# Lightning attention and a GELU MLP on one core: the first four MLP blocks by single chunks, VectorE rounding the first weights, chunk 2 transposed behind them

## The chip, the cores and the metric

The kernel runs on one NeuronCore of one Trainium2 chip. The metric is the time on the device in microseconds (us). TensorE (PE) multiplies matrices, VectorE (DVE) and ScalarE (ACT) work element by element and empty the accumulators (PSUM), GpSimd (POOL) issues the loads that change the type from f32 to bf16 and does a few products, SyncE (SP) issues the other transfers.

## The reference

Linear attention with a decay per head, in blocks of 64 rows, and then an MLP with an exact GELU over all heads of a token:

```python
    for b in range(nb):
        intra = np.einsum('bhic,bhjc->bhij', qb, kb) * Dmask[None]
        intra = np.einsum('bhij,bhjd->bhid', intra, vb)
        inter = np.einsum('bhid,bhde->bhie', qb * lam_pow[None], kv_state)
        out[:, :, sl] = intra + inter
        kv_state = lam_block[None, :, None, None] * kv_state + np.einsum('bhsd,bhse->bhde', kb_dec, vb)
    ...
    h = x @ w_in
    g = 0.5 * h * (1.0 + erf(h * inv_sqrt2))
    return (g @ w_out).astype(np.float32)
```

q, k and v are 4 x 8 x 768 x 64 (batch, heads, rows, width); x is 3072 x 512, w_in 512 x 2048, w_out 2048 x 512, all f32.

## The kernel before

The rows are cut into chunks of 128 rows of one batch with all heads: 24 chunks, numbered so that chunks 0 to 3 are the first rows of the four batches. Four chunks make a group; there are six groups. For each chunk k and q are transposed on PE (`transposed`, L165), their product gives the scores (`scores`, L191), DVE multiplies these by a mask that holds the decay (`masked`, L202), and the product with v gives the attention's output (`outputs`, L222), which ACT or DVE copies as bf16 into the chunk's 128 columns of the group's `x_t` (`empty_outputs`, L237). `next_state` (L206) multiplies k by the decayed v (`decay_v`, L160, on POOL) and DVE makes the state for the next chunk of that batch from it; its accumulator has the tag "t", of which there is one bank.

The MLP of a group (`mlp_blocks`, L398) is a list of blocks. A first-layer block `mm1(kf, ks, cols)` makes, for `ks` slices of 128 of the 2048 hidden columns, the product of w_in with the columns `cols` of `x_t`, four matmuls of that width for each slice, into a bank with the tag "mh" (two of them, shared with the transposes of k), and ACT applies GELU from there. In group 0 the plan (L437 to L440) goes by what of x exists: blocks of two chunks first, then the third alone, then three chunks, the fourth alone, and four. `group0` (L546) says before which block a step of attention stands; PE executes all in the order in which it is written. The head (L481 to L516) does chunks 0 and 1 and chunk 2's transposes; between the steps it has products of zeros (`keep_warm`, L465) that nobody reads, in a bank with the tag "mo" (two, shared with the transposes of q).

The order on the queues matters too. POOL issues the loads in the order of L94 (`k0 q0 v0 k1 q1 v1 w1 k2 ...`, where w1 to w7 are pairs of slices of w_in), then the decayed v of chunks 0 to 2, w_out and the further loads. The first two slices of w_in come another way: SP loads them as f32 into `wide_w` (L75), and ACT rounds them into `w_in_t` (L500). On DVE, the decay table (L125), its mask (L479, `causal`), the copies of transposes out of PSUM and the masked scores follow each other in the order of the text.

Behind group 0's first layer stand its second layer (L421), between whose parts the attention of chunks 4 to 7 lies (`e + 8` to `e + 15`), and DVE's sums of w_out (`w_out_sums`, L263), which the later groups use.

Of the kernel before, what the change touches and what calls it, by code (L numbers as in the profile page):

```python
# [15 lines left out]
def kernel(  # L16
# [10 lines left out]
    nc = tc.nc  # L27
# [3 lines left out]
    C = 128  # L31
# [8 lines left out]
    M = 4  # L40
# [33 lines left out]
    wide_w = sum_pool.tile([128, NK1, 256], F32, tag="g1", name="wide_w")  # L74
# [7 lines left out]
    w_in_t = w_pool.tile([128, NK1, d_ff], BF16)  # L82
# [65 lines left out]
    xT = {}  # L148
    states = {}

    def bank(shape, dtype, tag, name):
        return ps.tile(shape, dtype, tag=tag, name=name, bufs=2 if tag in ("sc", "mh", "mo") else 1)
# [12 lines left out]
    def transposed(c, name, tag, empty):  # L165

        src, t_ps = getattr(c, name), bank([128, HP, C], BF16, tag, "t_ps")
        for hp in range(HP):
            nc.tensor.transpose(t_ps[:, hp, :], src[:, 2 * hp:2 * hp + 2, :], ident)  # L169
        dst = work_pool.tile([128, HP, C], BF16, tag=name + "T", name=name + "T")  # L170
        setattr(c, name + "T", dst)
        empty(dst, t_ps)  # L172
# [18 lines left out]
    def scores(c):  # L191
        sc_ps = [bank([128, HP, C], F32, "sc", f"sc_ps{hi}") for hi in range(2)]
        for hp in range(HP):
            for hi in range(2):
                p = slice(hi * D, (hi + 1) * D)
                nc.tensor.matmul(sc_ps[hi][:, hp, :], c.kT[p, hp, :], c.qT[p, hp, :], start=True, stop=True)  # L196
        c.sc_m = work_pool.tile([128, HP, 2, C], BF16, tag="sc_m", name="sc_m")
        c.sc_ps = sc_ps
        for hi in range(0 if c.n == 0 else 2):
            masked(c, hi)  # L200

    def masked(c, hi):  # L202
        mask = decay[:, hi] if c.early else cmask[:, None, :].to_broadcast((128, HP, C))
        nc.vector.tensor_mul(c.sc_m[:, :, hi, :], c.sc_ps[hi], mask)  # L204

    def next_state(c):  # L206
        if c.sb == NB - 1:
            return
        kv_ps = bank([128, HP, 128], F32, "t", "kv_ps")
        for hp in range(HP):  # L210
            nc.tensor.matmul(kv_ps[:, hp, :], c.k[:, 2 * hp:2 * hp + 2, :], c.v_dec[:, 2 * hp:2 * hp + 2, :],  # L211
                             start=True, stop=True)
        new = work_pool.tile([128, HP, 128], BF16, tag="state_f", name="state", bufs=8)
        if c.sb == 0:
            nc.vector.tensor_mul(new, kv_ps, lam_blk)
        else:
            tmp = work_pool.tile([128, HP, 128], F32, tag="tmp", name="tmp")
            nc.vector.tensor_add(tmp, kv_ps, states[c.n])  # L218
            nc.vector.tensor_mul(new, tmp, lam_blk)  # L219
        states[c.n + M] = new  # L220

    def outputs(c, x_t, off, evacuate=True):  # L222
        o_ps = bank([128, HP, C], F32, "o", "o_ps")
        if c.sb > 0:
            for hp in range(HP):
                nc.tensor.matmul(o_ps[:, hp, :], states[c.n][:, hp, :], c.qT[:, hp, :],  # L226
                                 start=(hp == 0), stop=False, skip_group_check=True)
        v = c.v if c.early else c.v_dec
        for hi in range(2):
            for hp in range(HP):  # L230
                nc.tensor.matmul(o_ps[hi * D:(hi + 1) * D, hp, :], v[:, 2 * hp + hi, :], c.sc_m[:, hp, hi, :],  # L231
                                 start=(c.sb == 0 and hp == 0), stop=True, skip_group_check=True)
        c.x_o, c.o_ps = x_t[:, :, off * C:(off + 1) * C], o_ps
        if evacuate:
            empty_outputs(c)

    def empty_outputs(c):  # L237
        if c.n < 2 * M:
            nc.scalar.copy(c.x_o, c.o_ps)
        else:  # L240
            nc.vector.tensor_mul(c.x_o, c.o_ps, lam_q)  # L241
# [151 lines left out]
        blocks += [((lambda f=f, u=u: f(u)), KH * DH) for f in (m3, m4, m5, m2, m1, m6, m7) for u in range(2)]  # L393
        return blocks

    N1 = 21

    def mlp_blocks(g):  # L398
        T = M * C
        x_t = xT[g]  # L400
        g_t = g_pool.tile([128, NK2, T], BF16, tag="g", name="g_t")

        def mm1(kf, ks=1, cols=slice(0, T)):
            n = cols.stop - cols.start

            def run():
                h_ps = bank([128, ks, n], F32, "mh", "h_ps")
                parts = [(0, T - C), (T - C, T)] if g == 1 and kf == 0 else [(0, n)]
                for k in range(ks):
                    for lo, hi in parts:  # L410
                        for ki in range(NK1):
                            nc.tensor.matmul(h_ps[:, k, lo:hi], w_in_t[:, ki, (kf + k) * 128:(kf + k + 1) * 128],  # L412
                                             x_t[:, ki, cols.start + lo:cols.start + hi],
                                             start=(k == 0 and lo == 0 and ki == 0), stop=(ki == NK1 - 1),
                                             skip_group_check=True)
                nc.scalar.activation(g_t[:, kf:kf + ks, cols], h_ps, ACT.Gelu)  # L416
            return run

        om = {}

        def mm2(io, part):  # L421
            def run():
                if part == 0:
                    om[io] = bank([128, d_model], F32, "mo", "o2_ps")
                for kf in range(part * 4, part * 4 + 4):
                    nc.tensor.matmul(om[io], g_t[:, kf, io * C:(io + 1) * C], w_out_t[:, kf, :],  # L426
                                     start=(kf == 0), stop=(kf == NK2 - 1))
                if part == NK2 // 4 - 1:
                    o_sb = out_pool.tile([128, d_model], F32, tag="o_s", name="o_sb")
                    nc.scalar.copy(o_sb, om[io])  # L430
                    nc.sync.dma_start(out_r[g, :, io, :], o_sb)
            return run

        parts = NK2 // 4
        if g > 0:
            return blocks_by_seven(g, g_t, [(mm1(kf), 4 * T) for kf in range(NK2)])
        two, three, third, fourth = slice(0, 2 * C), slice(0, 3 * C), slice(2 * C, 3 * C), slice(3 * C, T)  # L437
        plan = [(kf, 1, two) for kf in range(6)] + [(0, 4, third), (4, 2, third)]
        plan += [(kf, 1, three) for kf in range(6, 12)] + [(kf, 4, fourth) for kf in range(0, 12, 4)]
        plan += [(kf, 1, slice(0, T)) for kf in range(12, NK2)]  # L440
        assert len(plan) == N1
        blocks = [(mm1(kf, n, cols), 4 * n * (cols.stop - cols.start)) for kf, n, cols in plan]
        blocks += [(mm2(io, part), 4 * 512) for pair in range(0, M, 2) for part in range(parts)
                   for io in (pair, pair + 1)]
        return blocks
# [15 lines left out]
    live = {}  # L461
# [3 lines left out]
    def keep_warm(n, new=True, cols=256):  # L465

        if new:
            idle_ps[0] = bank([128, 512], F32, "mo", "idle_ps")
        for _ in range(n):
            nc.tensor.matmul(idle_ps[0][:, :cols], idle[:, :128], idle[:, :cols], start=True, stop=True)  # L470

    def early(n):
        live[n] = begin(n, early=True)
        return live[n]

    copy = nc.vector.tensor_copy
# [4 lines left out]
    make_powers()  # L481
    nc.scalar.activation(warm, pos, ACT.Gelu)
    keep_warm(11, cols=512)
    c = early(0)
    causal(0)
    transposed(c, "k", "mh", copy)
# [7 lines left out]
    c = early(1)  # L494
# [2 lines left out]
    keep_warm(3, new=False)  # L497
    transposed(c, "q", "mo", copy)
    outputs(live[0], xT[0], 0)
    nc.scalar.copy(w_in_t[:, :, :256], wide_w)  # L500
    keep_warm(2)
    scores(c)
    keep_warm(9, new=False)
    make_lam_blk()
    outputs(live[1], xT[0], 1)
    c = early(2)
    transposed(c, "k", "mh", copy)
    transposed(c, "q", "mo", copy)
    keep_warm(1)
    for n in range(3):  # L510
        decay_v(live[n], nc.gpsimd)
    for s in range(2):
# [28 lines left out]
    def both_transposed(c):  # L541
        transposed(c, "k", "mh", nc.vector.tensor_copy)
        transposed(c, "q", "mo", nc.vector.tensor_copy)

    e = N1
    group0 = {  # L546
        1: [lambda: scores(live[2])],
        5: [lambda: outputs(live[2], xT[0], 2)],
        6: [lambda: next_state(live[0])],
        7: [lambda: next_state(live[1])],  # L550
        8: [lambda: both_transposed(live[3])],
        9: [lambda: next_state(live[2])],
        10: [lambda: scores(live[3])],
        12: [lambda: outputs(live[3], xT[0], 3)],
        17: [lambda: next_state(live[3])],
        e: [w_out_sums, lambda: decay_v(live[4], nc.vector)],
        e + 8: [lambda: transposes(live[4])],
        e + 9: [lambda: scores(live[4])],
# [10 lines left out]
    for n in range(2 * M, NCH):  # L569
        g, i = n // M - 1, n % M  # L570
        first, apart = (0.21, 0.2) if g == 1 else (0.06, 0.245)
# [65 lines left out]
```

## Time and profile before

| what | value |
|---|---|
| time, median of 3 runs | 209.86 us (209.69 to 210.2) |
| profiled execution, its own time | 209.99 us |
| its span in the profile | 208.2 us |
| PE busy | 200.3 us, 96% of the span |
| granted PE clock | 0.998 |
| POOL's issue of a load of k, q or v | about 0.9 us, 128 KB each |

A line of the timeline gives the start, the length, the engine, the line of the kernel, the operation with what it writes and reads, the count, and in brackets how long the engine had been idle and what ended that. Matmuls overlap, so the time from one start to the next is what one costs, and not its length. In the chain of waits each step is followed back to what released it.

### The profile page before, as it was taken

What the parts mean: (1) busy time and instruction counts of PE and PEld (TensorE: products, weight loads), DVE (VectorE), ACT (ScalarE), POOL (GpSimd) and SP (SyncE); (2) the same over time, 40 slices, a digit from 0 to 9 for tenths busy, and PEclk for the clock granted to TensorE, in tenths of its full rate; (3) what the DMA queues carried; (4) which work ended last, traced back from release to release, by engine and by line L of the source; (5) the groups of instructions that cost most, each with busy time, mean ns of one, the idle gap of its engine ahead of it and who ended that gap; (6) DMA issues with size and microseconds to landing.
All of it is one profiled execution on the core that took longest, in us unless ns stands there. A gap on an engine that the chain in (4) does not pass through costs nothing.

```text
span 208.2 us, 4142 instructions
## 1 busy us (share of the span) xinstructions
PE 200.3 (96%) x1708; PEld 130.5 (63%) x1725; DVE 139.0 (67%) x220; ACT 81.7 (39%) x145; POOL 97.1 (47%) x112
## 2 busy tenths in 40 slices
PE   7889999999999999999999999999999999999992
PEld 2457574465555788654688554688555688544881
DVE  4744525855476789889779689579678579123482
ACT  4966563324555410265420265410365410466200
POOL 8999953799998995499300493000200000000000
PEclk9999999999999999999999999999999999999999
DMA  5999999999999999999930699100651000500014
GB/s 116 155 174 177 200 207 188 154 215 148 151 177 154 153 150 154 233 141 175 155 25 3 219 134 175 29 0 3 227 103 29 0 0 3 201 0 0 3 50 151
DMA packets 102370, 24.65 MB, mean 118 GB/s; under 512 B 92880, under 2 KB 99536, under 8 KB 102352
## 3 DMA queue, kind: packets, MB, share of 16 engines
q0 software_dynamic: 80688, 13.37, 90.2%
q1 hardware_dynamic: 21664, 11.02, 23.5%
q8 instruction: 13, 0.21, 0.4%
q14 instruction: 5, 0.04, 0.1%
HBM read 27.27 MB, written 6.29 MB: 161 GB/s over the span
## 4 chain that ended last, share of the span: by engine, by line
PE 86%; POOL 8%; DVE 3%; issue 1%; POOLq 0%; DVEq 0%
PE h_ps L412 39%; PE p_ps L306 9%; PE r_ps L306 8%; PE q_ps L306 8%; PE o_ps L426 7%; PE o_ps L231 4%; PE s_ps L306 3%; PE sc_ps L196 3%; PE kv_ps L211 3%; POOL w_in_t L88 3%; PE o_ps L226 2%; POOL k_t L67 2%; POOL q_t L67 2%; POOL v_t L67 2%; PE t_ps L169 1%
## 5 line engine op out<-in xcount | busy, mean ns | idle before, releaser
L416 ACT ACTIVATE g_t<-h_ps 128x512 bf16<-128x512 f32 (+2 forms) x101 | 58.2, 576 | 81.2 <-PE h_ps L412 81.0
L412 PE MATMUL h_ps<-x_t,w_in_t 128*128 128x512 bf16 (+3 forms) x446 | 88.7, 343 | 0.6
L412 PEld LDWEIGHTS <-w_in_t 128*128 128x128 bf16 x460 | 40.2, 98 | 36.0 <-issue 0.6
L163 POOL TENSOR_TENSOR v_dec<-v_t,lam_m 128x512 bf16<-128x512 bf16 x23 | 25.2, 1101 | 44.5 <-PE kv_ps L211 42.9
L306 PEld LDWEIGHTS <-g_sum 128*128 128x128 bf16 x400 | 38.6, 98 | 5.2
L281 DVE TENSOR_TENSOR g_sum<-g_t 128x1024 bf16<-128x1024 bf16 x50 | 33.6, 716 | 11.3 <-ACT g_t L416 11.3
L204 DVE TENSOR_TENSOR sc_m<-sc_ps,cmask 128x512 bf16<-128x512 f32 x40 | 25.6, 680 | 2.0 <-PE sc_ps L196 2.0
L67 POOL DMA_DIRECT2D v_t<-in_v_dram x24 | 21.4, 893 | 3.3 <-DMA w_out_t<-in_moe_w_out_dram 2.9
L67 POOL DMA_DIRECT2D k_t<-in_k_dram x24 | 22.2, 924 | 1.7 <-DMA w_out_t<-in_moe_w_out_dram 1.4
L67 POOL DMA_DIRECT2D q_t<-in_q_dram x24 | 21.6, 898 | 2.1 <-DMA w_out_t<-in_moe_w_out_dram 2.1
L306 PE MATMUL r_ps<-w_sum,g_sum 128*128 128x256 bf16 x160 | 19.3, 273 | 0.1
L241 DVE TENSOR_TENSOR x_t<-o_ps,lam_q 128x512 bf16<-128x512 f32 x16 | 11.0, 687 | 10.2 <-PE o_ps L231 10.2
L306 PEld LDWEIGHTS <-g_t 128*128 128x128 bf16 x160 | 15.3, 98 | 3.2
L218 DVE TENSOR_TENSOR tmp<-kv_ps,state 128x512 f32<-128x512 f32 x16 | 11.0, 689 | 7.8 <-PE kv_ps L211 7.8
L426 PE MATMUL o_ps<-w_out_t,g_t 128*128 128x512 bf16 x61 | 14.8, 380 | 0.1
L219 DVE TENSOR_TENSOR state<-tmp,lam_blk 128x512 bf16<-128x512 f32 x16 | 14.4, 901 | 0.5
L306 PE MATMUL p_ps<-w_sum,g_t 128*128 128x256 bf16 x80 | 10.1, 273 | 0.0
L196 PE MATMUL sc_ps<-qT,kT 64*128 64x128 bf16 x192 | 9.5, 218 | 0.3 <-DVE qT L172 0.3
L306 PE MATMUL q_ps<-w_sum,g_t 128*128 128x256 bf16 x80 | 9.7, 273 | 0.0
L470 PE MATMUL idle_ps<-idle 128*128 128x256 bf16 (+1 forms) x33 | 8.4, 393 | 1.2 <-DVE idle L101 1.2
L426 PEld LDWEIGHTS <-g_t 128*128 128x128 bf16 x64 | 5.8, 98 | 6.1
L306 PE MATMUL p_ps<-w_out_t,g_sum 128*128 128x256 bf16 x80 | 9.6, 273 | 0.0
(65 smaller groups left out, 168.0 us busy)
## 6 DMA issues: line engine op xcount, KB each, us to landing
out_dram<-o_sb SPq DMA_DIRECT2D x9, 512.0 KB, 2.8
k_t<-in_k_dram POOLq DMA_DIRECT2D x24, 128.0 KB, 5.9
q_t<-in_q_dram POOLq DMA_DIRECT2D x24, 128.0 KB, 6.1
v_t<-in_v_dram POOLq DMA_DIRECT2D x24, 128.0 KB, 6.2
w_out_t<-in_moe_w_out_dram POOLq DMA_DIRECT2D x4, 512.0 KB, 11.1
w_in_t<-in_moe_w_in_dram POOLq DMA_DIRECT2D x7, 256.0 KB, 7.5
out_dram<-o_sb SPq DMA_DIRECT2D x5, 256.0 KB, 5.7
wide_w<-in_moe_w_in_dram SPq DMA_DIRECT2D x1, 512.0 KB, 4.2
```

Of the source, the lines that this page charges most:

```text
L67: nc.gpsimd.dma_start(raw[n, name], chunk_of(name, n))
L163: eng.tensor_mul(c.v_dec, c.v, lam_m[:, :, None].to_broadcast((128, H, D)))
L196: nc.tensor.matmul(sc_ps[hi][:, hp, :], c.kT[p, hp, :], c.qT[p, hp, :], start=True, stop=True)
L204: nc.vector.tensor_mul(c.sc_m[:, :, hi, :], c.sc_ps[hi], mask)
L218: nc.vector.tensor_add(tmp, kv_ps, states[c.n])
L219: nc.vector.tensor_mul(new, tmp, lam_blk)
L241: nc.vector.tensor_mul(c.x_o, c.o_ps, lam_q)
L281: nc.vector.tensor_tensor(gsum[i][:, ks, :], g_t[:, ka + k:ka + k + n4, ta], g_t[:, kb + k:kb + k + n4, tb], op=op)
L306: nc.tensor.matmul(o, left[i](k, slice(u * C, (u + 1) * C)), right[i](k), start=(begin and k == 0), stop=(k == KH - 1), skip_group_check=True)
L412: nc.tensor.matmul(h_ps[:, k, lo:hi], w_in_t[:, ki, (kf + k) * 128:(kf + k + 1) * 128], x_t[:, ki, cols.start + lo:cols.start + hi], start ...
L416: nc.scalar.activation(g_t[:, kf:kf + ks, cols], h_ps, ACT.Gelu)
L426: nc.tensor.matmul(om[io], g_t[:, kf, io * C:(io + 1) * C], w_out_t[:, kf, :], start=(kf == 0), stop=(kf == NK2 - 1))
```

## The change

The plan of group 0 begins with blocks of one chunk: two of two slices for the first chunk, one of four slices for the second; the blocks of two chunks are left for slices 4 and 5. The plan has 20 blocks in place of 21. Block 0 now stands before chunk 1's outputs, and block 1 behind them. Chunk 2 is transposed behind block 2, and its scores stand before block 3. The idle matmuls are 15 in these places, where there were 10. The rounding of `wide_w` is a DVE copy ahead of chunk 0's transposes, and no longer an ACT copy behind chunk 0's outputs. Of the steps further on, the first state now stands behind the third chunk's block of four slices (it stood ahead of it) and the second behind the third chunk's block of two slices, right ahead of chunk 3's transposes; the others keep their place in the work, by the new numbers of blocks.

```diff
-    N1 = 21
+    N1 = 20
...
-        two, three, third, fourth = slice(0, 2 * C), slice(0, 3 * C), slice(2 * C, 3 * C), slice(3 * C, T)
-        plan = [(kf, 1, two) for kf in range(6)] + [(0, 4, third), (4, 2, third)]
+        two, three = slice(0, 2 * C), slice(0, 3 * C)
+        first, second, third, fourth = (slice(i * C, (i + 1) * C) for i in range(M))
+        plan = [(0, 2, first), (2, 2, first), (0, 4, second)] + [(kf, 1, two) for kf in range(4, 6)]
+        plan += [(0, 4, third), (4, 2, third)]
...
     keep_warm(11, cols=512)
+    copy(w_in_t[:, :, :256], wide_w)
     c = early(0)
...
     outputs(live[0], xT[0], 0)
-    nc.scalar.copy(w_in_t[:, :, :256], wide_w)
     keep_warm(2)
     scores(c)
-    keep_warm(9, new=False)
     make_lam_blk()
-    outputs(live[1], xT[0], 1)
-    c = early(2)
-    transposed(c, "k", "mh", copy)
-    transposed(c, "q", "mo", copy)
-    keep_warm(1)
+    early(2)
...
-        1: [lambda: scores(live[2])],
-        5: [lambda: outputs(live[2], xT[0], 2)],
+        0: [lambda: keep_warm(2)],
+        1: [lambda: keep_warm(2), lambda: outputs(live[1], xT[0], 1)],
+        3: [lambda: both_transposed(live[2]), lambda: keep_warm(5), lambda: scores(live[2]),
+            lambda: keep_warm(6, new=False)],
+        4: [lambda: outputs(live[2], xT[0], 2)],
         6: [lambda: next_state(live[0])],
-        7: [lambda: next_state(live[1])],
-        8: [lambda: both_transposed(live[3])],
-        9: [lambda: next_state(live[2])],
-        10: [lambda: scores(live[3])],
-        12: [lambda: outputs(live[3], xT[0], 3)],
-        17: [lambda: next_state(live[3])],
+        7: [lambda: next_state(live[1]), lambda: both_transposed(live[3])],
+        8: [lambda: next_state(live[2])],
+        9: [lambda: scores(live[3])],
+        11: [lambda: outputs(live[3], xT[0], 3)],
+        16: [lambda: next_state(live[3])],
```

## The prediction, made before the changed kernel ran

> **What bounds the kernel now.** The page comes first: the engines' shares and the chain that ended last.
>
> ```profile
> PE 200.3 (96%) x1708; PEld 130.5 (63%) x1725; DVE 139.0 (67%) x220; ACT 81.7 (39%) x145; POOL 97.1 (47%) x112
> PE 86%; POOL 8%; DVE 3%; issue 1%; POOLq 0%; DVEq 0%
> ```
>
> TensorE (PE) carries the chain but for 8% of POOL, which is the head: the chain in order of time runs over POOL's load issues from 1.38 us to the end of the first decayed v at 18.53, and on PE from there. So the edits count by what they do to PE's order of work in the head, and a change there is worth what is left of it at the next point that does not move with PE. Next the timeline of PE, from 10.8 to 22 us (start, length, engine, line, what, count, idle before):
>
> ```profile
> 11.04 1.16 PE L470 MATMUL idle_ps<-idle 128*128 128x256 bf16 x9
> 12.12 0.74 PE L231 MATMUL o_ps<-sc_m,v_t 128*64 128x128 bf16 x8
> 13.42 0.40 PE L169 MATMUL t_ps<-ident,k_t 128*128 128x128 bf16 x4 [0.56 <-DMA k_t<-in_k_dram]
> 14.25 0.40 PE L169 MATMUL t_ps<-ident,q_t 128*128 128x128 bf16 x4 [0.44 <-DMA q_t<-in_q_dram]
> ...
> 18.79 1.06 PE L412 MATMUL h_ps<-x_t,w_in_t 128*128 128x128 bf16 x16
> 19.81 0.40 PE L211 MATMUL kv_ps<-v_dec,k_t 128*128 128x128 bf16 x4
> 20.04 0.61 PE L412 MATMUL h_ps<-x_t,w_in_t 128*128 128x128 bf16 x8
> 20.53 0.38 PE L169 MATMUL t_ps<-ident,k_t 128*128 128x128 bf16 x4
> 20.75 0.39 PE L169 MATMUL t_ps<-ident,q_t 128*128 128x128 bf16 x4
> 21.12 0.81 PE L412 MATMUL h_ps<-x_t,w_in_t 128*128 128x384 bf16 x4
> ```
>
> The hole that the change fills is seen here: from 11.04 to 14.60 PE does nine idle matmuls, chunk 1's outputs and chunk 2's transposes, and waits 1.0 us for k and q of chunk 2. The mark to measure against is 21.12, the first block of three chunks: up to there both orders hold the same useful work (blocks 0 to 5 for two chunks, the same six for the third, two states, chunk 3's transposes), and behind it they go on alike.
>
> Then the timelines of DVE and ACT, which set when PE's inputs are there:
>
> ```profile
> 4.16 1.29 DVE L125 TENSOR_TENSOR decay<-dist,ln 128x512 f32<-128x512 f32 x2 [1.69 <-ACT ln L121]
> 6.10 0.69 DVE L479 TENSOR_TENSOR decay<-decay,cmask 128x512 f32<-128x512 f32 x1 [0.65 <-ACT decay L126]
> 6.71 0.42 DVE L172 COPY kT<-t_ps 128x512 bf16<-128x512 bf16 x1
> 7.59 0.42 DVE L172 COPY qT<-t_ps 128x512 bf16<-128x512 bf16 x1 [0.46 <-PE t_ps L169]
> ...
> 11.14 1.29 DVE L204 TENSOR_TENSOR sc_m<-sc_ps,decay 128x512 bf16<-128x512 f32 x2 [0.58 <-PE sc_ps L196]
> ```
>
> ```profile
> 10.99 1.05 ACT L500 CAST w_in_t<-wide_w 128x1024 bf16<-128x1024 f32 x1
> 11.94 0.81 ACT L143 COPY lam_blk<-lam_c 64x256 f32<-64x256 f32 x2
> 12.90 0.59 ACT L239 CAST x_t<-o_ps 128x512 bf16<-128x512 f32 x1
> ```
>
> DVE has 0.65 and 0.46 us of slack early on, and the second part of x is there at 13.49.
>
> Last, what does not move with PE (timeline of all engines around 40 us):
>
> ```profile
> 39.57 0.69 DVE L163 TENSOR_TENSOR v_dec<-v_t,lam_m 128x512 bf16<-128x512 bf16 x1 [0.16 <-DMA v_t<-in_v_dram]
> 40.18 0.68 DVE L175 TENSOR_TENSOR qT<-t_ps,lam_q 128x512 bf16<-128x512 bf16 x1
> 40.91 0.40 PE L196 MATMUL sc_ps<-qT,kT 64*128 64x128 bf16 x8
> ```
>
> Chunk 4's scores start 0.05 after qT is done at 40.86; qT stands behind a decayed v that waited for a load, and DVE's eight sums of w_out before it run without a pause from 34.40, when w_out landed. PE is ready at about 40.9 as well (the matmul before is issued at about 40.59 and takes 0.22 to the next, and a change to this form costs 0.09). So whatever PE gains before that is lost in front of these scores; what it loses is kept.
>
> **The change, part by part.** Start to start on PE, read off the rows: 0.056 us for a matmul of 128 columns, 0.109 for 256, 0.22 for four transposes; 0.33 to 0.35 for eight of scores or outputs with the change of form around them.
>
> *Rounding on DVE.* 128x1024 f32 to bf16. No such copy is in the trace: from below, twice the PSUM copies of 512 (0.42, of which 0.34 to the next) make 0.7 to 0.8, and 0.69 if only the part by element doubles; from above, f32 products run 0.69 and 0.60 more per 512, so 1.29. I take 0.75: one source, as the copy has. It starts at 5.45, when the decay products are done; wide_w is then there (issued 1.20, 4.2 to landing: 5.40). At 0.75 it ends at 6.20 and moves the mask product by 0.1, at 1.29 by 0.6; kT's copy follows, and qT's waits for q until 7.59 anyway, so 0.46 more of slack: nothing, or 0.1 at the upper end. Without that cover it would cost its whole length, as all of DVE up to the mask of chunk 0 stands behind it. On ACT 1.05 us falls away at 10.99; nothing waited for ACT there.
>
> *Blocks 0 to 2.* Chunk 1's scores leave PE at 11.04 as before. Two idle matmuls (0.23), block 0 (8 x 0.056 = 0.45; x's first part is done at 11.10), two idle ones: 11.94. Chunk 1's outputs wait for the second mask at 12.43, as before, and leave PE at 12.80. Block 1 needs w_in's second load (6.77 + 5.8 = 12.57): 13.25. Block 2 needs x's second part, 13.49: it starts at 13.55, waits 0.30, and ends at 14.44 (16 x 0.056).
>
> *Chunk 2.* Transposes 14.47 to 14.92 (k and q are there by 14.21); DVE's two copies end at 15.67. Five idle matmuls end at 15.5, scores start at 15.73 (wait 0.23) against 15.17 before. Six idle matmuls: 16.73. Block 3 (4 x 0.109 = 0.44, its load there at 10.13 + 6.3 = 16.43): 17.16. Outputs wait for the mask (16.15 + 1.29 = 17.44) and leave PE at 17.84. Block 4: 18.28. Block 5 reads x's third part: ACT copies it from 17.94 to 18.53, so 18.59 (wait 0.31) to 19.48.
>
> *States and chunk 3.* First state's matmuls 19.48 to 19.71; its v came at 18.53. Block 6 (0.45): 20.16. The second state needs the one kv bank, which DVE frees 0.69 after 19.98, at 20.67: 20.73 (wait 0.57; before, a block of 16 lay between and the wait was 0.1). With its four and the eight transposes: 21.41, and the first block of three chunks at 21.44.
>
> **The sum:** 21.44 - 21.12 = **+0.3 us**. Of the hole's idle time, five more idle matmuls (15 for 10, 0.55) and four new waits (0.30 + 0.23 + 0.31 + 0.57 = 1.41) take back all that the early blocks win. Behind 21.4 the loads leave room (the w_in load for blocks 8 and 9 is issued at 14.21 and takes 7.5: 21.7, needed at 23.4), and the order is the old one. At 40.9 up to 0.05 of it goes unseen. The profiled execution took 209.99 (span 208.2 and 1.8 around it), 0.13 above the median of the three, 209.86; the span becomes 208.5, and against the median I say **210.15**.
>
> **A rule against it.** The row: DVE and POOL do hold each other up in this trace; a sum of g took 1.40 for its usual 0.68 at 77.48, while POOL multiplied v from 77.26 to 78.32. POOL's issue of k at 1.38 took 1.06 for the later 0.88 to 0.90, beside DVE's constants. The Trainium skill (SBUF — State Buffer, section on SBUF's two separate sides) says that an f32 copy within SBUF on VectorE locks GpSimd out of a shared port, so that a DMA issued by GpSimd cannot write its descriptors. By that rule the time would be that of the first rival below. By another of its pages (VectorE: DVE Perf Modes, the perf-mode tier table) 2048 such elements take 1.23 us, so that some 0.7 is an estimate for 1024; the sum would be the same.
>
> **Rivals.**
> *POOL held by the copy (slower).* The copy runs in the middle of POOL's issue of chunk 1's q and v (5.05 and 5.91, 0.9 each, back to back). q lands at 9.65 (4.6 after its issue) and is transposed at 9.70: no slack; chunk 1's scores and outputs, x's second part and block 2 all hang on it, and later loads queue behind. If POOL stands for the copy's length, all moves by up to 0.75, the loads before 40.9 too: 209.86 + 0.3 + 0.3 to 0.75 = 210.5 to 210.9, say **210.75**. It decides from about 0.35 us of stall. For it: the rows above. Against: issue runs 4.6 us ahead of landing, so the transfers may have enough queued.
> *The copy comes late (slower at the edge).* wide_w is 0.05 ahead of its use; 0.3 later and 1.29 long, the copy ends near 7.0, qT's comes 0.3 later and masks and outputs with it: **210.4**.
> *The waits do not arise (faster).* Were the four waits absent, PE would reach the mark at 20.35, 0.8 early: **209.1**. That needs the loads of w_out and v before 40.9 to come earlier too, or the gain stays in front of chunk 4's scores; the row of 39.57 speaks against it.
>
> **How the numbers follow.** Forecast 0.46, its own range 209.8 to 210.5; POOL held 0.30; copy late 0.10; faster 0.14. A measurement of this kernel can tell about 0.3% (0.63 us) from no change: faster is under 209.23, slower over 210.49. Faster 0.13 (nearly all of its rival), slower 0.34 (most of POOL held, half of copy late, little of the forecast), same 0.53. The range, 209.2 to 210.95, leaves out the far half of each side's rival.
>
> **What would show it.** The first block of three chunks at 21.4; waits of PE ahead of block 2, block 5, chunk 2's scores and the second state near 0.3, 0.3, 0.2 and 0.6; DVE's copy at 5.45 and 0.7 to 0.8 long; POOL's issues at 5.05 and 5.91 still 0.9. Wrong if these issues last over 1.2, if chunk 1's q is transposed after 10.0, or if chunk 4's scores start before 40.8.

## The result, and the profile after

| kernel | median, us | lowest to highest | middle half of the runs |
|---|---|---|---|
| before (22 runs) | 209.89 | 209.66 to 210.54 | 209.75 to 209.97 |
| changed (22 runs) | 210.38 | 209.89 to 211.87 | 210.11 to 210.60 |

The ratio is 1.0025, with an interval of 1.0013 to 1.0037: 0.5 us slower (0.3 to 0.8), which is under the 0.3% that was named as the bound of "same". What the medians do not say is in the last column: in these runs the changed kernel scatters twice as much. The profiled execution of the changed kernel is one of its quickest, 209.99 with a span of 208.2, as before; that of the kernel before lies a little above its median. So the two profiles cannot show the difference of the medians.

PE's timeline after the change, for the stretch that was shown of before:

```profile
10.64 0.40 PE L196 MATMUL sc_ps<-qT,kT 64*128 64x128 bf16 x8
10.97 0.39 PE L472 MATMUL idle_ps<-idle 128*128 128x256 bf16 x2
11.20 0.61 PE L412 MATMUL h_ps<-x_t,w_in_t 128*128 128x128 bf16 x8
11.64 0.38 PE L472 MATMUL idle_ps<-idle 128*128 128x256 bf16 x2
11.96 0.84 PE L231 MATMUL o_ps<-sc_m,v_t 128*64 128x128 bf16 x8
12.87 1.65 PE L412 MATMUL h_ps<-x_t,w_in_t 128*128 128x128 bf16 x24
14.36 0.39 PE L169 MATMUL t_ps<-ident,k_t 128*128 128x128 bf16 x4
14.58 0.39 PE L169 MATMUL t_ps<-ident,q_t 128*128 128x128 bf16 x4
14.81 0.71 PE L472 MATMUL idle_ps<-idle 128*128 128x256 bf16 x5
15.59 0.40 PE L196 MATMUL sc_ps<-qT,kT 64*128 64x128 bf16 x8
15.92 0.83 PE L472 MATMUL idle_ps<-idle 128*128 128x256 bf16 x6
16.77 0.61 PE L412 MATMUL h_ps<-x_t,w_in_t 128*128 128x256 bf16 x4
17.31 0.43 PE L231 MATMUL o_ps<-sc_m,v_t 128*64 128x128 bf16 x8
17.67 1.81 PE L412 MATMUL h_ps<-x_t,w_in_t 128*128 128x256 bf16 x20
19.32 0.39 PE L211 MATMUL kv_ps<-v_dec,k_t 128*128 128x128 bf16 x4
19.54 0.61 PE L412 MATMUL h_ps<-x_t,w_in_t 128*128 128x128 bf16 x8
20.56 0.40 PE L211 MATMUL kv_ps<-v_dec,k_t 128*128 128x128 bf16 x4 [0.41 <-DVE state L215]
...
21.24 0.81 PE L412 MATMUL h_ps<-x_t,w_in_t 128*128 128x384 bf16 x4
```

The hole after 11 us is filled, and another has opened: between chunk 2's transposes and block 3 (14.81 to 16.77) PE does eleven idle matmuls and the scores, where the kernel before did a block, the scores and then four blocks of two chunks, which covered the masks of DVE. The second state waits for the kv bank: eight matmuls from 19.54 need 0.45, the state starts at 20.56. The first block of three chunks, the mark, comes at 21.24 for 21.12; counted from chunk 1's scores it is 10.60 us for 10.41.

DVE's and POOL's timelines around the copy:

```profile
5.33 1.13 DVE L486 CAST w_in_t<-wide_w 128x1024 bf16<-128x1024 f32 x1
6.38 0.67 DVE L481 TENSOR_TENSOR decay<-decay,cmask 128x512 f32<-128x512 f32 x1
6.97 0.41 DVE L172 COPY kT<-t_ps 128x512 bf16<-128x512 bf16 x1
7.47 0.42 DVE L172 COPY qT<-t_ps 128x512 bf16<-128x512 bf16 x1
```

```profile
5.03 0.90 POOL L67 DMA_DIRECT2D q_t<-in_q_dram  x1
5.90 1.04 POOL L67 DMA_DIRECT2D v_t<-in_v_dram  x1
6.92 0.77 POOL L88 DMA_DIRECT2D w_in_t<-in_moe_w_in_dram  x1
```

The copy is long (1.13), the mask product behind it comes at 6.38 for 6.10, and qT's copy finds its slack and is not late. POOL's issue of chunk 1's v takes 1.04 for 0.91.

Why the two profiled executions have the same span although the mark is 0.12 later is seen in DVE's timeline at 77 us, first before, then after:

```profile
77.48 1.40 DVE L281 TENSOR_TENSOR g_sum<-g_t 128x1024 bf16<-128x1024 bf16 x1
...
82.40 0.67 DVE L376 TENSOR_TENSOR f_x<-f_x,r_ps 128x512 f32<-128x512 f32 x1
```

```profile
77.61 0.68 DVE L281 TENSOR_TENSOR g_sum<-g_t 128x1024 bf16<-128x1024 bf16 x1
...
81.81 0.67 DVE L376 TENSOR_TENSOR f_x<-f_x,r_ps 128x512 f32<-128x512 f32 x1
```

The sum of g met POOL's product of v before (1.40) and did not after (0.68). DVE's last step, for which PE waits, ends 0.6 earlier, and PE's next product starts at 83.06 for 83.12: that execution got back 0.18 there. The experiments below bear this out: from chunk 4's scores to that product it takes 42.21 to 42.32 in the five profiles in which this sum met the product of v in full (before, e6, e8, e9, e11), and 42.03 to 42.05 in the eight others, e5 left aside. Four of the five have the order of before, seven of the eight that of the changed kernel; whether the order brings this about was not tried.

### The profile page after: what moved, and what is told of

Its sections match the earlier page's. It is cut to its first block, busy times and chain, and to the rows that moved or that the text cites. A ratio compares the mean times of both kernels' runs of the same rounds, so it can differ in the third digit from the quotient of the medians.

```text
span 208.2 us, 4199 instructions
## 1 busy us (share of the span) xinstructions
PE 200.9 (96%) x1746; PEld 131.0 (63%) x1746; DVE 141.8 (68%) x221; ACT 80.6 (39%) x143; POOL 97.2 (47%) x112
## 3 DMA queue, kind: packets, MB, share of 16 engines
q0 software_dynamic: 80688, 13.37, 92.5%
q1 hardware_dynamic: 21664, 11.02, 23.2%
## 4 chain that ended last, share of the span: by engine, by line
PE 91%; DMA 3%; POOL 3%; DVE 1%; ACT 0%; issue 0%; POOLq 0%; DVEq 0%
PE h_ps L412 40%; PE r_ps L306 9%; PE p_ps L306 9%; PE q_ps L306 8%; PE o_ps L426 7%; PE s_ps L306 4%; PE o_ps L231 4%; PE sc_ps L196 4%; DMA w_in_t<-in_moe_w_in_dram 3%; PE kv_ps L211 2%; PE o_ps L226 2%; PE t_ps L169 1%; POOL k_t L67 1%; POOL v_t L67 1%; POOL q_t L67 1%
## 5 line engine op out<-in xcount | busy, mean ns | idle before, releaser
L412 PE MATMUL h_ps<-x_t,w_in_t 128*128 128x512 bf16 (+3 forms) x476 | 90.2, 338 | 0.2
L281 DVE TENSOR_TENSOR g_sum<-g_t 128x1024 bf16<-128x1024 bf16 x50 | 34.9, 743 | 10.7 <-ACT g_t L416 10.7
L219 DVE TENSOR_TENSOR state<-tmp,lam_blk 128x512 bf16<-128x512 f32 x16 | 15.0, 939 | 0.5
L426 PE MATMUL o_ps<-w_out_t,g_t 128*128 128x512 bf16 x64 | 15.3, 380 | 0.0
```

Of the source, the lines that this page charges most:

```text
L281: nc.vector.tensor_tensor(gsum[i][:, ks, :], g_t[:, ka + k:ka + k + n4, ta], g_t[:, kb + k:kb + k + n4, tb], op=op)
```

## The experiments

Theory 1: the DVE copy holds POOL, and the blocks hang on the loads behind it. Theory 2: PE's new order costs, the copy nothing. Theory 3, formed after the first four kernels: the kernel before hides delays of the head in waits that end when a load or POOL is done; the changed one hands them on. "Mark" is the start of the first block of three chunks. The kernel before has a median of 209.84 to 209.88 in the three sets, beside the same kernels. The ratios and intervals are those on record, to the kernel before; a ratio need not be that of the two medians, as a few runs far out count in it.

**e1: the rounding back on ScalarE.** The changed kernel, with

```diff
     nc.scalar.activation(warm, pos, ACT.Gelu)
+    nc.scalar.copy(w_in_t[:, :, :256], wide_w)
     keep_warm(11, cols=512)
-    copy(w_in_t[:, :, :256], wide_w)
```

> The changed kernel with one part moved: ScalarE rounds wide_w, right behind its warm-up GELU at 9.9 us, and DVE does not. Theory 1 (the DVE copy holds POOL's issue, and blocks 1 and 3 hang on the loads behind it): POOL's issue of chunk 1's v is back at 0.91 us (1.04 in the changed kernel), w_in's second load lands near 12.5 (12.8), the third near 16.4 (16.7), block 3 starts at 16.5 or before; the first block of three chunks at 21.0 (21.24); the time 0.2 to 0.4 us below the changed kernel's 210.4, with less scatter. Theory 2 (only PE's new order costs; the copy is free): the loads land as in the changed kernel, or sooner without PE following; time within 0.1 of 210.4.

Median 210.34, ratio to before 1.0023 (1.0001 to 1.0045), mark at 21.23. POOL's issue is back at 0.91, and the time has not followed. In this execution w_in's second load, on which block 1 hangs, also landed 1.0 us sooner (issued at 6.78 and 5.0 us on its way, for 6.92 and 5.9), and the mark stayed.

**e2: the DVE copy alone, in the kernel before.**

```diff
     keep_warm(11, cols=512)
+    copy(w_in_t[:, :, :256], wide_w)
...
-    nc.scalar.copy(w_in_t[:, :, :256], wide_w)
```

> The kernel before, with one part of the change alone: DVE rounds wide_w ahead of chunk 0's transposes, ScalarE does not. Theory 1: POOL's issue of chunk 1's v takes 1.0 us or more, loads from there on land 0.2 to 0.3 later, chunk 2's transposes (which wait for k and q at 13.4 and 14.25) move by as much, and the first block of three chunks comes at 21.3 to 21.4 for 21.12: time 210.1 to 210.3. Theory 2: nothing moves by more than 0.1; time 209.8 to 210.0.

Median 209.96, ratio 1.0003 (0.9972 to 1.0033), mark at 21.13. The issue is 1.04 long here too. The interval is wide, but e1 and e2 agree: theory 1 falls. PE's timeline of e2 showed something else:

```profile
13.68 0.40 PE L169 MATMUL t_ps<-ident,q_t 128*128 128x128 bf16 x4 [0.39 <-DMA q_t<-in_q_dram]
...
18.57 0.38 PE L211 MATMUL kv_ps<-v_dec,k_t 128*128 128x128 bf16 x4 [0.63 <-POOL v_dec L163]
...
21.13 0.81 PE L412 MATMUL h_ps<-x_t,w_in_t 128*128 128x384 bf16 x4
```

In this execution chunk 2's q came 0.57 earlier than in the profile of before (13.68 for 14.25), and nothing came of it: the first state waited for POOL until 18.57, the same time as before. Hence theory 3.

**e3: without the eleven idle matmuls.** The changed kernel, with

```diff
-        3: [lambda: both_transposed(live[2]), lambda: keep_warm(5), lambda: scores(live[2]),
-            lambda: keep_warm(6, new=False)],
+        3: [lambda: both_transposed(live[2]), lambda: scores(live[2])],
```

> The changed kernel without the five and the six idle matmuls around chunk 2's scores (nothing else). Theory 1: block 3 waits for w_in's third load, which lands at 16.7, so it still starts at 16.75 and the time stays at 210.3 to 210.5. Theory 2 (the idle matmuls stand on the path): block 3 starts at 16.05 and the mark comes 0.3 to 0.6 earlier; time 209.8 to 210.1. If the granted clock falls below 0.99 in the first 20 us, the idle matmuls were needed and neither can be read.

Median 210.10, ratio 1.0011 (0.9987 to 1.0035), granted clock 1.0. In the profiled execution PE waits in place of doing the idle matmuls, 0.62 for DVE's copies ahead of the scores and 0.73 for the load ahead of block 3, and the mark stays (21.25):

```profile
16.76 0.61 PE L412 MATMUL h_ps<-x_t,w_in_t 128*128 128x256 bf16 x4 [0.73 <-DMA w_in_t<-in_moe_w_in_dram]
```

So here the load bounds block 3, as expected by theory 1, but it does not bound the mark. In all seven profiles with this order up to there, e5 left aside (the changed kernel, e1, e3, e4, e7, e10, e11), block 4 starts 2.07 to 2.08 after chunk 2's scores, whether block 3 starts 0.76 (e11) or 1.18 (the changed kernel) after them: chunk 2's outputs behind block 3 wait for DVE's masks. The idle matmuls and the load both fit into that wait. The median lies at the upper edge of what theory 2 expected, and the mark where theory 1 had it; the interval is too wide for the median to decide.

**e4: the states' order.** The changed kernel, with

```diff
-        7: [lambda: next_state(live[1]), lambda: both_transposed(live[3])],
-        8: [lambda: next_state(live[2])],
-        9: [lambda: scores(live[3])],
+        7: [lambda: both_transposed(live[3]), lambda: next_state(live[1])],
+        9: [lambda: next_state(live[2]), lambda: scores(live[3])],
```

> The changed kernel with the order around the states changed: chunk 3's transposes ahead of the second state, the third state one block later, right ahead of chunk 3's scores. Theory 2 (the wait of 0.58 us of the second state for the one kv bank is on the path): the wait falls under 0.15, the first block of three chunks comes at 20.8 for 21.24, and the time falls by 0.3 to 0.45 to about 210.0. Rival (what PE gains before 40.9 us is lost in front of chunk 4's scores or in the DVE stretch at 76 to 83): the mark moves the same, the time by less than 0.15.

Median 210.19, ratio 1.0004 (0.998 to 1.0028). In the profiled execution chunk 1's scores came at 11.11, 0.47 later than in the changed kernel, and the mark at 21.28, 0.04 later: 10.17 between them for 10.60, so 0.43 of the wait of 0.57 is won. Not all of it lasts, first e4, then the changed kernel:

```profile
23.01 0.69 DVE L215 TENSOR_TENSOR state<-kv_ps,lam_blk 128x512 bf16<-128x512 f32 x1 [0.62 <-PE kv_ps L211]
23.62 1.28 DVE L204 TENSOR_TENSOR sc_m<-sc_ps,decay 128x512 bf16<-128x512 f32 x2
...
25.27 4.24 PE L412 MATMUL h_ps<-x_t,w_in_t 128*128 128x384 bf16 x56
```

```profile
23.29 1.29 DVE L204 TENSOR_TENSOR sc_m<-sc_ps,decay 128x512 bf16<-128x512 f32 x2 [0.28 <-PE sc_ps L196]
...
24.95 4.24 PE L412 MATMUL h_ps<-x_t,w_in_t 128*128 128x384 bf16 x56
```

The third state now stands right ahead of chunk 3's scores, so DVE makes it before chunk 3's masks. These come 0.72 after the scores (22.90) for 0.43 (22.86), and the block behind chunk 3's outputs starts 3.99 after the mark for 3.71: 0.28 is lost again. That leaves 0.15, and from chunk 1's scores to the end of the span it is 197.4 for 197.6. The median is 0.2 under the changed kernel's 210.38, which was measured in another set; the interval is too wide to show that. e11 and e12 have this order of the states too.

**e5 and e11: both edits together**, twice (the first in a set with much scatter: there the kernel before had its middle half from 209.72 to 210.42).

> The changed kernel with both: no idle matmuls around chunk 2's scores, and chunk 3's transposes ahead of the second state with the third state one block later. Theory (PE's new order is what costs; the wait for the kv bank, 0.58, and idle matmuls where w_in's third load is there early): the wait of the second state is gone, 8 matmuls of the first block of three chunks start at 20.8 at the latest for 21.24 in the changed kernel (counted from chunk 1's scores at 10.64), time 209.8 to 210.1. Rival (gains before 40.9 us are lost in front of chunk 4's scores): as in the run with the state order alone, 210.1 to 210.4.

> The changed kernel without the eleven idle matmuls and with the states in the other order, once more, because its first runs fell on a chip with much scatter. Theory (PE's order is the cost): 0.3 to 0.5 below the changed kernel's median on this chip. Rival (the loads are the cost, and no order behind chunk 2's scores mends it): within 0.15 of it.

e5: median 210.41, ratio 1.0024 (0.9998 to 1.0051); its profile fell on an execution of 212.72 in which chunk 0's q came 1.5 us late and the granted clock was 0.980, so the order can't be read from it. e11: 210.25, ratio 1.0012 (0.9998 to 1.0026), 0.2 below the changed kernel beside it (e10); between theory and rival. Its mark is at 21.03, 10.32 after chunk 1's scores. Its block 3 waited for its load until 16.43, which cost nothing at block 4, and chunk 3's q was transposed at 20.58, 0.14 later behind its k than in e4.

**e10: the changed kernel once more**, beside e9, e11 and e12.

> The changed kernel once more, beside the next three on one chip: the mark for them. Theory 3 (its head hands every delay of the loads on): 210.2 to 210.6, and wider scatter than the kernel before on the same chip.

Median 210.46, ratio 1.0033 (1.0012 to 1.0053). The middle half is 210.21 to 210.67, that of the kernel before beside it 209.69 to 210.06: wider, but not twice as wide. This execution's head is 0.29 later than that of the first profile, and so is what follows up to the mark:

```profile
10.93 0.40 PE L196 MATMUL sc_ps<-qT,kT 64*128 64x128 bf16 x8
...
15.88 0.40 PE L196 MATMUL sc_ps<-qT,kT 64*128 64x128 bf16 x8
...
20.84 0.40 PE L211 MATMUL kv_ps<-v_dec,k_t 128*128 128x128 bf16 x4 [0.41 <-DVE state L215]
...
21.52 0.81 PE L412 MATMUL h_ps<-x_t,w_in_t 128*128 128x384 bf16 x4
```

**e6 and e7: four idle matmuls ahead of the first state**, in the kernel before (e6) and in the changed one (e7).

```diff
-        6: [lambda: next_state(live[0])],
+        6: [lambda: keep_warm(4), lambda: next_state(live[0])],
```

> The kernel before with four idle matmuls (0.44 us) right ahead of the first state. Theory 3 (the kernel before has slack there: its first state waits for POOL's decayed v, which ends near 18.5 whatever PE does, and so hides what comes late in the head): 0.2 or more of the 0.44 is hidden; first state at 18.8, time 209.95 to 210.15. Rival (no slack): the first state 0.44 later, time 210.3.

> The changed kernel with four idle matmuls (0.44 us) right ahead of the first state. Theory 3 (the changed kernel gets there 0.8 after POOL's decayed v and has no slack): all of it shows, first block of three chunks at 21.65 for 21.24, time 210.7 to 210.9. Rival (as much slack as before): 210.4 to 210.6.

e6: median 210.15, ratio 1.0005 (0.9989 to 1.002). Chunk 1's scores came at 11.12 (10.71 in the profile of before) and there are 0.44 us of idle matmuls, yet the first state starts at 18.54 and the mark is at 21.09: the wait for chunk 2's loads had shrunk to 0.40, and the wait ahead of the state was gone.

```profile
14.01 0.40 PE L169 MATMUL t_ps<-ident,q_t 128*128 128x128 bf16 x4 [0.40 <-DMA q_t<-in_q_dram]
...
18.54 0.39 PE L211 MATMUL kv_ps<-v_dec,k_t 128*128 128x128 bf16 x4
```

In part this was the landing: chunk 2's q came 0.24 earlier than in the profile of before (14.01 for 14.25). With it at 14.25 the same rows give the first state at 18.78, as expected, so that half of the 0.44 is hidden by the wait for POOL. e7: median 211.08, ratio 1.0071 (1.0043 to 1.0099), scores at 10.79, mark at 21.81: 11.02 between them, the changed kernel's 10.60 and all of the 0.44. Theory 3 holds in both profiles. The medians say less: e6's is 0.28 above the kernel before beside it (209.87), at the upper edge of what was expected, and e7's is 0.6 to 0.7 above the changed kernel's (210.46 in e10, 210.38), more than the 0.44 and over what was expected, in the same set as e5.

**e8 and e9: POOL's wait taken out of the kernel before.** DVE makes the decayed v of chunks 0 and 1 (e8) or of chunk 0 alone (e9), behind chunk 2's masks; e9:

```diff
-    for n in range(3):
+    for n in (1, 2):
         decay_v(live[n], nc.gpsimd)
...
         1: [lambda: scores(live[2])],
+        2: [lambda: decay_v(live[0], nc.vector)],
```

> The kernel before with the decayed v of chunks 0 and 1 made by DVE, behind chunk 2's masks (DVE stands idle from 16.9 to 19.06), and not by POOL, which so issues w_out's loads about 2 us sooner. Theory 3: the first state no longer waits (0.22 in the profile before), the first block of three chunks comes 0.1 to 0.3 earlier, and as the head's delays are no longer hidden the scatter grows; time 209.6 to 209.85. Rival (a further point, chunk 4's scores or the DVE stretch at 76 to 83, sets the time): 209.85 to 210.0.

> The kernel before with DVE making the decayed v of chunk 0 alone (in the run with two of them the second state waited 0.83 for DVE). Theory 3 (POOL's decayed v is the point that sets the head of the kernel before): first state at 17.6 to 18.0 for 18.57, second state without a wait over 0.2, first block of three chunks at 20.1 to 20.6 for 21.12, unless q of chunk 3, landing at 19.4 to 19.9, holds its transposes; time 209.1 to 209.6. Rival (chunk 4's scores near 40.9 set the time): 209.7 to 209.95, with PE waiting there.

e8: median 209.72, ratio 0.9985 (0.9962 to 1.0008), mark at 20.89, as expected; the second state then waited for DVE (0.66). The scatter did not grow: the middle half is 209.59 to 210.18, in the set in which the kernel before had 209.72 to 210.42. e9: median 209.48, middle half 209.40 to 209.56, but two runs at 211.8 leave the ratio at 0.9996 (0.997 to 1.0023). Nine of the twelve runs are quicker than every one of the 35 of the kernel before beside them (209.65). PE's timeline of e9:

```profile
17.71 0.39 PE L211 MATMUL kv_ps<-v_dec,k_t 128*128 128x128 bf16 x4
...
18.95 0.40 PE L211 MATMUL kv_ps<-v_dec,k_t 128*128 128x128 bf16 x4
...
20.27 0.81 PE L412 MATMUL h_ps<-x_t,w_in_t 128*128 128x384 bf16 x4
...
40.17 0.40 PE L196 MATMUL sc_ps<-qT,kT 64*128 64x128 bf16 x8
```

The first state is 0.86 earlier and the mark 0.85. The span is 0.6 shorter (207.6): in front of chunk 4's scores PE now waits some 0.1 for qT (done at 40.11), and the sum of g at 76.75 met POOL again (1.50).

**e12: blocks in the waits only.** The changed kernel, with the second chunk's block in halves, one between chunk 2's two transposes and one behind them, and the states in e4's order:

```diff
-        plan = [(0, 2, first), (2, 2, first), (0, 4, second)] + [(kf, 1, two) for kf in range(4, 6)]
+        plan = [(0, 2, first), (2, 2, first), (0, 2, second), (2, 2, second)] + [(kf, 1, two) for kf in range(4, 6)]
...
+        2: [lambda: transposed(live[2], "k", "t", copy)],
+        3: [lambda: transposed(live[2], "q", "mo", copy)],
+        4: [lambda: scores(live[2])],
+        5: [lambda: outputs(live[2], xT[0], 2)],
+        7: [lambda: next_state(live[0])],
+        8: [lambda: both_transposed(live[3]), lambda: next_state(live[1])],
+        10: [lambda: next_state(live[2]), lambda: scores(live[3])],
```

> The changed kernel with its blocks put into the waits only: the second chunk's block in two halves, one between chunk 2's two transposes and one behind them (k's transposes in the kv bank's tag), so that chunk 2's scores come as early as before; no idle matmuls there; chunk 3's transposes ahead of the second state, the third state right ahead of chunk 3's scores. Theory (the changed kernel lost because work that stood in the wait behind chunk 2's scores was moved ahead of them): scores of chunk 2 at 15.1 to 15.3 for 15.59, first block of three chunks at 20.3 to 20.6 for 21.24, time 209.4 to 209.8. Rival (the loads or chunk 4's scores take it back): 209.85 or more.

Median 209.91, ratio 0.9997 (0.9984 to 1.001): 0.55 under the changed kernel beside it, and level with the kernel before. The profiled execution, of 209.45 and a span of 207.7, is the third quickest of the twelve. In it chunk 2's scores come at 15.03, the mark at 20.46, and then PE stands at the load of block 4:

```profile
16.39 0.61 PE L412 MATMUL h_ps<-x_t,w_in_t 128*128 128x256 bf16 x4 [0.96 <-DMA w_in_t<-in_moe_w_in_dram]
```

## Why the prediction was right, and what its sum left out

**The order on PE: right, and to 0.1 us where it can be read.** The four waits, from the rows of the changed profile: ahead of chunk 2's scores 0.23, as forecast (15.59, with the five idle matmuls issued by 14.81 + 5 x 0.109 = 15.36); ahead of block 5 0.32 for 0.31 (from 17.67 four matmuls of 256 and sixteen of 128 columns need 1.33, the next row starts 1.65 later); ahead of the second state 0.57, as forecast. The fourth was put at block 2, for x's second part, at 0.30; there it was 0.15 (from 12.87, 24 x 0.056 = 1.34, the next row is at 14.36), and block 1 had waited for its load, as the chain of waits of that profile shows:

```profile
6.92 5.90 DMA w_in_t<-in_moe_w_in_dram
12.87 1.65 PE h_ps L412 x24
```

The sum said 21.44 from scores at 10.71, which is 10.73; it was 10.60, in this and in the four other kernels with this order (e1 10.59, e3 10.58, e10 10.59, e7 10.58 without its idle matmuls). e4 shows one of the waits as time: 0.43 of the way to the mark, of which its order of the states loses 0.28 again.

One term of the sum's account was no cost: the five more idle matmuls, put at 0.55. e3 leaves out eleven of them, and the mark stays at 10.58 from the scores; they stand inside the waits and only fill them.

**The copy: nothing, as forecast, by the cover that was named.** It took 1.13 for the 0.75 that I chose, near the upper bound of 1.29; the slack ahead of qT's copy took it up. e1 differs from the changed kernel, and e2 from the kernel before, by no more than 0.1 in the median. The first rival (POOL held) falls by its own condition: POOL's issue was 0.13 longer, under the 0.35 from which that case was to decide. The second, a late copy, fell too: wide_w was there. By the Trainium skill's rule on the port (SBUF — State Buffer, section on SBUF's two separate sides) POOL could not have written its descriptors while the copy ran; the trace shows 0.13 on one of the two issues beside it, not the length of the copy. That rule is for a copy in one of the faster modes, and whether this one, with 1.13 for an estimated 0.7, ran in such a mode no run here shows.

**The size: 0.3 said, 0.5 measured, and that they lie so close is in part luck.** The sum was about PE's order, and of that the first two profiles show 0.12 at the mark, 0.19 counted from chunk 1's scores. The rest of the 0.5 must come from something that the sum did not have. It was made on one execution, and took the head's loads as fixed. They are not: chunk 1's scores, which follow the landing of chunk 0's and 1's loads, start between 10.59 and 11.12 in these profiles, and at 13.37 in e5's. In the kernel before, a late head can be taken up by the waits for chunk 2's k and q (1.0 us in its profile) and for POOL's decayed v: its order has the mark at 21.12, 21.13 and 21.09 (before, e2, e6) with scores at 10.71, 10.81 and 11.12. The prediction named these waits only as a hole to be filled; filling it removes the cover. In the five profiles with the changed order the mark is the scores plus 10.6, so that there a late head is handed on in full. The 22 runs fit that: the quickest of the two kernels differ by 0.23, about what the order costs, the first quarters by 0.36, the medians by 0.49 and the third quarters by 0.63. Even so, that the rest of the 0.5 is this handing on is inferred; no single run measures it, and the medians of e6 and e7, and the scatter in the later sets, bear it out only in part. Whether the meeting of DVE and POOL at 77 us plays into the medians stays open too.

**Faster, if the waits did not arise:** e12 takes most of them out. Counted from chunk 1's scores its mark is 0.81 earlier than before (9.60 for 10.41), as that rival priced it, but its median is 209.91 for 209.1. The price itself does not follow from the sum: the four waits make 1.41, so that without them the mark would be at 20.03, 1.1 early, and not at 20.35. Part of what e12 wins is lost by e4's order of the states: from the mark to chunk 4's scores e4, e11 and e12 need 20.05 for the changed kernel's 19.78. I put the point that takes it back at chunk 4's scores, at 40.9 and fixed. It moves: in the profile after, DVE's last eight sums of w_out began at 33.55 for 34.40 and the decayed v behind them at 38.72 for 39.57, and then DVE waited for PE's transposes (0.85), not PE for DVE. In e9 PE reached it at 40.1 and waited some 0.1; in e3 the sums began at 34.69 and the scores at 41.19, 19.94 after the mark, so that 0.16 was lost there. That step was too strong, and the mean over executions of what is lost there stays open.

## What to carry to other kernels

A wait for a load can also be a buffer: work that is put into it may be paid for by the delays that it used to hide, so look at what the engine waits for next and at the scatter, and not at the median alone. Moving work into one hole takes it out of another place; here the four blocks behind chunk 2's scores had covered the masks. To gain, shorten what the first wait that does not move with the engine hangs on: one 0.7 us product moved from POOL to DVE brought the mark 0.85 us forward in the profile and the median 0.36 down, though the interval of its ratio holds 1. And a step moved to win one wait (e4) can hold up the next engine: count what it puts ahead of the work behind it.

## What the runs showed of the hardware

The same loads, issued at the same times by POOL, take different times to land: chunk 1's q, issued at 5.0, took 4.5 to 5.0 us in thirteen of the fourteen profiles and 6.0 in that of e5; chunk 2's k, issued at 7.5 to 7.7, took 5.1 to 6.4. An f32 copy to bf16 of 128x1024 took DVE 1.06 to 1.14 us in the nine profiles that have it there, beside POOL's issue of chunk 1's v, which took 1.04 in each of them and 0.91 in the five others. ScalarE needs 1.05 (before) and 1.03 (e1) for the same copy. In e5's execution, of 212.72, the granted clock fell to 0.7 and 0.6 in the second and third of 40 slices:

```profile
PEclk9769999999999999999999999999999999999998
```

The idle matmuls of the head did not prevent it there; whether PE's wait of 1.72 for chunk 0's late q was the cause was not tried. The eleven that e5 leaves out stand later, around chunk 2's scores, and e3, which leaves out the same, kept a clock of 1.0.
